# One token tile transposed by a DMA from ScalarE's queue, with six feature tiles ahead of it

## The chip, the cores and the metric

The kernel runs on one core of a Trainium2 chip. The core has five engines with instruction streams of their own: TensorE (PE in the profile; its weight loads are PEld), VectorE (DVE), ScalarE (ACT), GpSimd (POOL) and SyncE (SP). SyncE, ScalarE and GpSimd each have a queue from which they issue DMAs. The metric is the device time in microseconds, as a median over runs.

## The reference

The input x has 2048 tokens of 512 features. It is normalised per token, and the result goes through a diagonal state space layer and a gated feed-forward layer. Both are added to x:

```python
xn = _layernorm(x)
# A: state space layer, P = 512 complex states
Lam_bar = exp(dt * Lam);  B_bar = ((Lam_bar - 1) / Lam)[:, None] * Bmat
Bu = einsum("bld,pd->blp", xn, B_bar)
h[t] = Lam_bar * h[t-1] + Bu[t]
A = 2 * einsum("blp,dp->bld", h, Cmat).real + xn * Dskip
# B: feed-forward layer, F = 1376 hidden features
B = (silu(xn @ w_gate) * (xn @ w_up)) @ w_down
out = x + A + B
```

Inputs and output are bfloat16.

## The kernel before

**Tiling.** The 2048 tokens are 4 chunks of 512, and a chunk is 4 token tiles of 128 (`TPC`). The 512 input features are 4 slices of 128 (`KD`), called k. The hidden features are 11 feature tiles, called fi, the last with 96 rows. Matmuls read `xnT`, the normalised tokens with the features on the partitions, so each token tile has to be transposed after its normalisation. PSUM has eight banks of 512 columns, all handed out by `bank()`.

**Two ways to transpose.** `xT_pe(n)` takes four 128x128 transposes on TensorE (L231) into two banks, and two copies from there into `xnT` by VectorE (L238) or ScalarE (L240). `xT_dma(n)` issues one transposing DMA from SyncE's queue (L245). The kernel uses `xT_pe` for token tiles 0 to 3 and `xT_dma` for 4 to 15.

**The order of the work** is written out by hand; each engine runs its instructions in program order. The start loads x and the first weights in groups of feature tiles (0 to 1, 2, 3 to 6, 7 to 9) from SyncE's queue, L121 to L135; x of chunk 1 follows (L137). After that come the eight transposing DMAs of the state space input matrix, `BT` (L140), four for its real part and four for its imaginary part, one for each k; the weights of feature tiles 7 to 9 stand between the two parts (L112, called from L142 and L143), and the weights of the last feature tile behind (L145, L146).

On TensorE the first chunk goes as follows. Ten dummy matmuls (L653) come first. Then token tiles 0 to 3 are normalised one by one (`norm_dve`, L214, on VectorE; its scale comes from ScalarE, L202) and transposed, and `head_mm` (L676) multiplies the tiles that have arrived with feature tiles 0 to 2 into six held banks. With tile 3 these banks are complete; `gu_out` (L455, L456) empties each pair on ScalarE, the gate through Silu and the up product by a copy. Feature tiles 3 to 6 follow for all 512 tokens at once (`gateup_tile`, whose matmuls are L441). Then comes `bproj_tile`, the product of the chunk with `BT` (L366): the four 128-state tiles of the real part, and then those of the imaginary part, each with the matmuls of k = 0 to 3 in turn. Feature tiles 7 to 10 close the chunk's gate and up products. The later chunks follow with the same stages, and the output products with `w_down` and with the state space output matrix.

VectorE's longer work (tables of sines and cosines, statistics of later chunks, rotations, scans) lies in a backlog. `pump(us)` behind a group of matmuls takes from it about as much as fits into the given time. The products of gate and up for a pair of feature tiles (L460) are collected in `products`, and `multiply(keep)` issues them.

Of the kernel before, what the change touches and what calls it, by code (L numbers as in the profile page):

```python
# [11 lines left out]
BF16 = mybir.dt.bfloat16  # L12
ALU = mybir.AluOpType
ACT = mybir.ActivationFunctionType
# [9 lines left out]
def kernel(  # L24
# [17 lines left out]
    nc = tc.nc  # L42
    _, L, D = A_x.shape
    Pst = A_Lambda_re.shape[0]
    F = B_w_gate.shape[1]
    assert L % 512 == 0 and D % 128 == 0 and Pst % 128 == 0 and Pst == D
    CW = 512
# [3 lines left out]
    TPC = CW // 128  # L51
    KD = D // 128
    NQ = Pst // 128
    FT = (F + 127) // 128
    fsz = [min(128, F - i * 128) for i in range(FT)]
# [3 lines left out]
    LA, LB = 32, 64  # L59
    FL = (FT - 1) * 128  # L60
# [6 lines left out]
    up_p = ctx.enter_context(tc.tile_pool(name="up_p", bufs=4))  # L67
# [5 lines left out]
    def bank(shape=(128, CW), dtype=F32):  # L73
        return psum.tile(list(shape), dtype, name="ps")
# [4 lines left out]
    x_v = A_x[0].rearrange("(n p) d -> p n d", p=128)  # L79
    out_v = out[0].rearrange("(n p) d -> p n d", p=128)  # L80
    wg_v = B_w_gate.rearrange("(k p) f -> p k f", p=128)
    wu_v = B_w_up.rearrange("(k p) f -> p k f", p=128)


    xall = const.tile([128, NT, D], BF16, name="xall")
    xnT = const.tile([128, KD, L], BF16, name="xnT")

    fgroups = [(0, 2), (2, 3), (3, 7), (7, FT - 1)]
    wg_g, wu_g = [], []
# [4 lines left out]
    w_last = const.tile([128, KD, 128], BF16, name="w_last")  # L94
    wu_last = const.tile([128, KD, LB], BF16, name="wu_last")
    wd_sb = const.tile([128, FT - 1, D], BF16, name="wd_sb")
    BT = const.tile([128, 2, KD, Pst], BF16, name="BT")
# [6 lines left out]
    def wslice(groups, fi, k):  # L104
        for (a, b), t in zip(fgroups, groups):
            if a <= fi < b:
                return t[:, k, (fi - a) * 128:(fi - a) * 128 + fsz[fi]]


    def load_w1(q, tiles, view, gi):  # L110
        a, b = fgroups[gi]
        q.dma_start(out=tiles[gi][:], in_=view[:, :, a * 128:min(F, b * 128)])  # L112
# [20 lines left out]
        nc.gpsimd.dma_start(out=prm_rows[i * NQ:(i + 1) * NQ, :], in_=v.rearrange("(q j) -> q j", j=128))  # L133
    load_w1(nc.sync, wg_g, wg_v, 2)
    load_w1(nc.sync, wu_g, wu_v, 2)  # L135
    for n in (TPC, TPC + 2):
        nc.sync.dma_start(out=xall[:, n:n + 2, :], in_=x_v[:, n:n + 2, :])  # L137
    for part, src in enumerate((A_B_re, A_B_im)):
        for k in range(KD):
            nc.sync.dma_start_transpose(out=BT[:, part, k, :], in_=src[:, k * 128:(k + 1) * 128])  # L140
        if part == 0:
            load_w1(nc.sync, wg_g, wg_v, 3)  # L142
            load_w1(nc.sync, wu_g, wu_v, 3)  # L143

    nc.sync.dma_start(out=w_last[:, :, 0:LB + LA], in_=wg_v[:, :, FL:F])  # L145
    nc.sync.dma_start(out=w_last[:, :, LB + LA:128], in_=wu_v[:, :, FL + LB:F])  # L146

    def load_late():
        nc.sync.dma_start(out=wu_last[:], in_=wu_v[:, :, FL:FL + LB])
# [43 lines left out]
    def xn_tile(c):  # L193
        return xn_end if c == NCH - 1 else xall[:, c * TPC:(c + 1) * TPC, :]
# [17 lines left out]
    def norm_dve(n, lo=0, hi=D):  # L212
        c, i = divmod(n, TPC)
        nc.vector.tensor_scalar(out=xn_tile(c)[:, i, lo:hi], in0=xall[:, n, lo:hi], scalar1=mv[:, n, 0:1],  # L214
                                scalar2=rstd[:, n:n + 1], op0=ALU.subtract, op1=ALU.mult)
# [8 lines left out]
    def xT_pe(n, on_dve=(), prm_too=False):  # L224

        c, i = divmod(n, TPC)
        for h in range(2):
            tp = bank((128, HK * 128 + 128), BF16)
            for k in range(HK):
                lo = (h * HK + k) * 128  # L230
                nc.tensor.transpose(out=tp[:, k * 128:(k + 1) * 128], in_=xn_tile(c)[:, i, lo:lo + 128],  # L231
                                    identity=ident[:])
            if prm_too and h == 1:
                prm_transpose(tp[:, HK * 128:])
            dst = xnT[:, h * HK:(h + 1) * HK, n * 128:(n + 1) * 128]
            src = tp[:, 0:HK * 128].rearrange("p (k t) -> p k t", k=HK)
            if h in on_dve:
                nc.vector.tensor_copy(out=dst, in_=src)  # L238
            else:
                nc.scalar.copy(out=dst, in_=src)  # L240
        return tp[:, HK * 128:]

    def xT_dma(n):
        c, i = divmod(n, TPC)
        nc.sync.dma_start_transpose(out=xnT[:, :, n * 128:(n + 1) * 128], in_=xn_tile(c)[:, i, :])  # L245


    prm = const.tile([128, 3, NQ], F32, name="prm")
# [9 lines left out]
    V = nc.vector  # L258

    def prm_transpose(pp):  # L260
        nc.tensor.transpose(out=pp, in_=prm_rows[:], identity=ident[:])
# [173 lines left out]
    u_pair = {}  # L435
    products = []

    def gu_mm(ps, groups, c, fi, lo, hi):
        fs = fsz[fi]
        for k in range(KD):  # L440
            nc.tensor.matmul(ps[:fs, lo:hi], lhsT=wslice(groups, fi, k),  # L441
                             rhs=xnT[:, k, c * CW + lo:c * CW + hi], start=(k == 0), stop=(k == KD - 1))

    def gu_tile(c):
        if c not in gu_tiles:
            gu_tiles[c] = gut.tile([128, FT - 1, CW], BF16, name="guT")
        return gu_tiles[c]

    def gu_out(c, fi, psg, psu):

        guT = gu_tile(c)
        fs = fsz[fi]
        if fi % 2 == 0:
            u_pair[c] = up_p.tile([128, 2, CW], BF16, name="u2")
        nc.scalar.activation(out=guT[:fs, fi, :], in_=psg[:fs], func=ACT.Silu)  # L455
        nc.scalar.copy(out=u_pair[c][:fs, fi % 2, :], in_=psu[:fs])  # L456
        if fi % 2 == 1:
            lo = fi - fi % 2
            g, u = guT[:fs, lo:fi + 1, :], u_pair[c][:fs, 0:fi - lo + 1, :]
            products.append(lambda: V.tensor_tensor(out=g, in0=g, in1=u, op=ALU.mult))  # L460

    up_last = {}

# [40 lines left out]
    def gateup_tile(c, fi):  # L504
        if fi == FT - 1:
            return gateup_last(c)
        psg = bank()
        gu_mm(psg, wg_g, c, fi, 0, CW)
        psu = bank()
        gu_mm(psu, wu_g, c, fi, 0, CW)  # L510
        gu_out(c, fi, psg, psu)
# [97 lines left out]
    def queue(tag, ops, at=None):  # L609
        ops = [[op[0], op[1], op[2] if len(op) > 2 else None, tag] for op in ops]  # L610
        if at is None:
            backlog.extend(ops)
        else:
            backlog[at:at] = ops

    def step():
        for item in backlog[0:AHEAD + 1]:
            if item[2] is not None:
                item[2]()
                item[2] = None  # L620
        cost, op, _, _ = backlog.pop(0)
        op()
        owed[0] -= cost

    def pump(us):

        owed[0] += us
        while backlog and owed[0] >= backlog[0][0] * 0.5:
            step()
        if not backlog:  # L630
            owed[0] = 0.0

    def multiply(keep):

        while len(products) > keep:
            products.pop(0)()
            owed[0] -= 0.65
# [7 lines left out]
    GU = 8 * 0.2163  # L645
    BP = 4 * 0.2163
    H = 3
    held = [(bank(), bank()) for _ in range(H)]
# [6 lines left out]
    def ln_rest(c, on_act):  # L655
        ops = [(0.7, lambda n=n: ln_stats(n)) for n in range(c * TPC, (c + 1) * TPC)]
        def fin():
            ln_rstd(c * TPC, (c + 1) * TPC)
        def nbf():
            ln_nb(c * TPC, (c + 1) * TPC)  # L660
        ops += [(0.1, fin)]
        tail = [(0.1, nbf)] if on_act else []
        for n in range(c * TPC, (c + 1) * TPC):
            def one(n=n):
                (norm_act if on_act else norm_dve)(n)
                xT_dma(n)
            tail.append((0.05 if on_act else 0.35, one))
        return ops, tail
# [3 lines left out]
    def head_mm(which, lo, hi, ks, fis):  # L672

        for fi in fis:
            for k in ks:
                nc.tensor.matmul(held[fi][which][:, lo * 128:hi * 128], lhsT=wslice((wg_g, wu_g)[which], fi, k),  # L676
                                 rhs=xnT[:, k, lo * 128:hi * 128], start=(k == 0), stop=(k == KD - 1))

    allk = range(KD)
# [31 lines left out]
    params_a(pp)  # L711
    head_mm(1, 0, 2, allk, (2,))
    norm_dve(3)
    head_mm(0, 2, 3, range(0, HK), range(H))
    head_mm(1, 2, 3, range(0, HK), range(H))
    xT_pe(3, on_dve=(0, 1))
    head_mm(0, 2, 3, range(HK, KD), range(H))
    head_mm(1, 2, 3, range(HK, KD), range(H))
    tables = table_ops()
# [3 lines left out]
    queue("tables", tables[2:3])  # L723
    queue("ln1", norm1)
    queue("tables", tables[3:4] + [(0.1, params_sin)] + tables[4:])
    for fi in range(H):
        head_mm(0, 3, 4, allk, (fi,))
        head_mm(1, 3, 4, allk, (fi,))
        gu_out(0, fi, *held[fi])
        pump(GU / 4)  # L730
    pump(2.0)

    def bproj_chunk(c):
        need(f"ln{c}")
# [47 lines left out]
        queue(f"ssm{c}", fwd + back)  # L782

    G0 = 7
    for fi in range(H, G0):
        gateup_tile(0, fi)
        pump(GU)
        multiply(1)
# [72 lines left out]
```

## Time and profile before

| | |
|---|---|
| median of 3 runs | 178.56 us (178.43 to 178.92) |
| the profiled execution | 178.79 us, its span 177.0 us |
| TensorE busy | 173.4 us |
| VectorE busy | 154.0 us |
| ScalarE busy | 94.2 us |
| GpSimd busy | 51.3 us |
| DMA, mean over the span | 92 GB/s, 16.23 MB |

The span is the stretch in which instructions run; the profiled execution's own time is 1.8 us longer. Times in the traces are counted from the span's start. In a timeline a row merges consecutive instructions of one line; its columns are start, duration, engine, line, operation, tiles, shapes and count. SPq and ACTq are the queues from which SyncE and ScalarE issue DMAs. A matmul's duration includes its way through the array; the distance between starts is what one costs in a row of them.

### The profile page before, as it was taken

What the parts mean: (1) busy time and instruction counts of PE and PEld (TensorE: products, weight loads), DVE (VectorE), ACT (ScalarE), POOL (GpSimd) and SP (SyncE); (2) the same over time, 40 slices, a digit from 0 to 9 for tenths busy, and PEclk for the clock granted to TensorE, in tenths of its full rate; (3) what the DMA queues carried; (4) which work ended last, traced back from release to release, by engine and by line L of the source; (5) the groups of instructions that cost most, each with busy time, mean ns of one, the idle gap of its engine ahead of it and who ended that gap; (6) DMA issues with size and microseconds to landing.
All of it is one profiled execution on the core that took longest, in us unless ns stands there. A gap on an engine that the chain in (4) does not pass through costs nothing.

```text
span 177.0 us, 2543 instructions
## 1 busy us (share of the span) xinstructions
PE 173.4 (98%) x927; PEld 82.3 (46%) x927; DVE 154.0 (87%) x234; ACT 94.2 (53%) x167; POOL 51.3 (29%) x85
## 2 busy tenths in 40 slices
PE   8999999999999999999999999999999999999993
PEld 2984444444444444444444444444444444444443
DVE  3789997999999996899999999999999999993033
ACT  3468898967299649923766661053866610001300
POOL 6050300000300050003999640058185250001410
PEclk9999999999999999999999999999999999999999
DMA  5998745996141016900000020019659600000662
GB/s 169 279 297 215 141 88 122 361 206 111 22 88 31 4 28 117 348 11 2 20 17 19 15 67 24 4 17 132 88 78 178 116 9 0 0 0 6 63 99 74
DMA packets 30764, 16.23 MB, mean 92 GB/s; under 512 B 19680, under 2 KB 30560, under 8 KB 30720
## 3 DMA queue, kind: packets, MB, share of 16 engines
q1 hardware_dynamic: 24704, 11.44, 27.9%
q0 software_dynamic: 5184, 4.07, 16.0%
q10 hardware_dynamic: 864, 0.56, 1.0%
q8 instruction: 7, 0.11, 0.3%
q14 instruction: 5, 0.04, 0.1%
HBM read 8.33 MB, written 5.24 MB: 77 GB/s over the span
## 4 chain that ended last, share of the span: by engine, by line
PE 96%; DMA 1%; DVE 1%; issue 0%
PE ps L441 36%; PE ps L587 16%; PE ps L366 16%; PE ps L575 10%; PE ps L549 10%; PE ps L676 3%; PE ps L496 2%; PE ps L538 2%; DMA xall<-in_A_x_dram 1%; PE ps L485 1%; PE ps L231 1%; DVE stats L197 0%; PE ps L653 0%; DVE xall L214 0%; DVE stats L684 0%; DVE res L592 0%
## 5 line engine op out<-in xcount | busy, mean ns | idle before, releaser
L441 PE MATMUL ps<-xnT,wu 128*128 128x512 bf16 x148 | 38.0, 379 | 0.0
L441 PE MATMUL ps<-xnT,wg 128*128 128x512 bf16 x148 | 38.0, 379 | 0.0
L408 DVE TENSOR_TENSOR_SCAN g<-r_t,car,u 128x512 bf16<-128x512 f32 x24 | 28.7, 1260 | 0.0
L455 ACT ACTIVATE guT<-ps 128x512 bf16<-128x512 f32 x40 | 24.4, 611 | 7.3 <-PE ps L441 5.5
L366 PE MATMUL ps<-xnT,BT 128*128 128x512 bf16 x128 | 28.3, 379 | 0.0
L587 PE MATMUL ps<-CF,wt 128*128 128x512 bf16 (+2 forms) x144 | 28.2, 356 | 0.0
L456 ACT CAST u<-ps 128x512 bf16<-128x512 f32 x40 | 23.9, 598 | 5.6 <-PE ps L441 5.6
L600 ACT CAST res<-ps 128x512 bf16<-128x512 f32 x12 | 6.7, 590 | 36.0 <-PE ps L587 26.8
L181 POOL DMA_DIRECT2D gu_rows<-ul x36 | 17.6, 498 | 18.1 <-DVE ul L473 18.1
L441 PEld LDWEIGHTS <-wu 128*128 128x128 bf16 x148 | 14.5, 98 | 17.4
L441 PEld LDWEIGHTS <-wg 128*128 128x128 bf16 x148 | 14.4, 98 | 17.2
L368 ACT CAST u<-ps 128x512 bf16<-128x512 f32 x32 | 18.4, 591 | 5.1 <-PE ps L366 4.9
L601 POOL DMA_DIRECT2D out_dram<-res x12 | 10.6, 1224 | 34.3 <-ACT res L600 34.2
L587 PEld LDWEIGHTS <-wt 128*128 128x128 bf16 x144 | 13.3, 98 | 15.0 <-issue 0.8
L366 PEld LDWEIGHTS <-BT 128*128 128x128 bf16 x128 | 12.5, 98 | 15.1
L206 POOL TENSOR_TENSOR rstd<-ve,neg_half 128x4 f32<-128x4 f32 x3 | 5.2, 1730 | 47.0 <-DVE ve L205 47.0
L575 PE MATMUL ps<-wd_sb,guT 128*128 128x512 bf16 x80 | 17.6, 379 | 0.0
L549 PE MATMUL ps<-wd_sb,guT 128*128 128x512 bf16 x80 | 17.4, 379 | 0.0
L460 DVE TENSOR_TENSOR guT<-guT,u 128x1024 bf16<-128x1024 bf16 x20 | 13.5, 678 | 0.0
L575 PEld LDWEIGHTS <-guT 128*128 128x128 bf16 x80 | 7.8, 98 | 9.4
L549 PEld LDWEIGHTS <-guT 128*128 128x128 bf16 x80 | 7.8, 98 | 9.5
L197 DVE BATCH_NORM_STATS2 stats<-xall 128x6 f32<-128x512 bf16 x14 | 9.5, 677 | 1.9 <-DMA xall<-in_A_x_dram 1.9
(114 smaller groups left out, 194.7 us busy)
## 6 DMA issues: line engine op xcount, KB each, us to landing
out_dram<-in_A_x_dram SPq DMA_DIRECT2D x1, 1536.0 KB, 7.1
out_dram<-res POOLq DMA_DIRECT2D x12, 128.0 KB, 3.5
out_dram<-xall POOLq DMA_DIRECT2D x3, 512.0 KB, 7.6
wd_sb<-in_B_w_down_dram SPq DMA_DIRECT2D x2, 640.0 KB, 9.0
xall<-in_A_x_dram SPq DMA_DIRECT2D x1, 1024.0 KB, 7.2
gu_rows<-ul POOLq DMA_DIRECT2D x36, 8.0 KB, 1.6
wg<-in_B_w_gate_dram SPq DMA_DIRECT2D x1, 512.0 KB, 5.0
wu<-in_B_w_up_dram SPq DMA_DIRECT2D x1, 512.0 KB, 6.1
```

The lines of the kernel that those rows point to most:

```text
L181: nc.gpsimd.dma_start(out=gu_rows[c][i * RT:(i + 1) * RT, p, :], in_=product[p * RT:(p + 1) * RT, i * 128:(i + 1) * 128])
L366: nc.tensor.matmul(ps[:], lhsT=BT[:, part, k, q * 128:(q + 1) * 128], rhs=xnT[:, k, c * CW:(c + 1) * CW], start=(k == 0), stop=(k == KD - 1))
L368: nc.scalar.copy(out=u_tiles[c][:, part, q, :], in_=ps[:])
L408: V.tensor_tensor_scan(out=g()[:, part, q, :], data0=r_t[:, q:q + 1].to_broadcast([128, CW]), data1=u_tiles[c][:, part, q, :], initial=ini ...
L441: nc.tensor.matmul(ps[:fs, lo:hi], lhsT=wslice(groups, fi, k), rhs=xnT[:, k, c * CW + lo:c * CW + hi], start=(k == 0), stop=(k == KD - 1))
L455: nc.scalar.activation(out=guT[:fs, fi, :], in_=psg[:fs], func=ACT.Silu)
L456: nc.scalar.copy(out=u_pair[c][:fs, fi % 2, :], in_=psu[:fs])
L460: products.append(lambda: V.tensor_tensor(out=g, in0=g, in1=u, op=ALU.mult))
L549: nc.tensor.matmul(o[:], lhsT=gu_tiles[k][:, fi, i * 128:(i + 1) * 128], rhs=wd_sb[:, fi, :], start=(fi == 0), stop=False)
L575: nc.tensor.matmul(o[:], lhsT=gu_tiles[c][:, fi, i * 128:(i + 1) * 128], rhs=wd_sb[:, fi, lo:hi], start=(fi == 0), stop=False)
L587: nc.tensor.matmul(o, lhsT=w_tiles[c][:, part, q, i * 128:(i + 1) * 128], rhs=CF[:, part, q, lo:hi], start=(fresh and part == 0 and q == 0 ...
L601: nc.gpsimd.dma_start(out=out_v[:, n, :], in_=res[:], accum_op=ALU.add)
```

## The change

Token tile 3 is no longer transposed by TensorE and copied by VectorE, but by one transposing DMA from ScalarE's queue. Feature tiles 0 to 5 (instead of 0 to 2) are multiplied with the first three token tiles, 384 columns, and their banks are emptied in this width. Then token tile 3 is multiplied with the same six feature tiles, four of them together in one bank each for gate and up, and two in a third bank; `end_out` empties these, and the products of the three pairs follow. The remaining feature tile 6 and the product with `BT` come after that as before.

The DMAs of `BT`, of the weights of feature tiles 7 to 9, and of the last feature tile's weights are put in a function, `load_mid`, which is called behind the transposing DMA of tile 3. They stay on SyncE's queue. The two loads of x for chunk 1 become one.

```diff
-    for n in (TPC, TPC + 2):
-        nc.sync.dma_start(out=xall[:, n:n + 2, :], in_=x_v[:, n:n + 2, :])
-    for part, src in enumerate((A_B_re, A_B_im)):
...
+    nc.sync.dma_start(out=xall[:, TPC:2 * TPC, :], in_=x_v[:, TPC:2 * TPC, :])
+
+    def load_mid():
+        for part, src in enumerate((A_B_re, A_B_im)):
+            for k in range(KD):
+                nc.sync.dma_start_transpose(out=BT[:, part, k, :], in_=src[:, k * 128:(k + 1) * 128])
+            if part == 0:
+                load_w1(nc.sync, wg_g, wg_v, 3)
+                load_w1(nc.sync, wu_g, wu_v, 3)
+        nc.sync.dma_start(out=w_last[:, :, 0:LB + LA], in_=wg_v[:, :, FL:F])
+        nc.sync.dma_start(out=w_last[:, :, LB + LA:128], in_=wu_v[:, :, FL + LB:F])
...
-    def xT_dma(n):
+    def xT_dma(n, q=nc.sync):
         c, i = divmod(n, TPC)
-        nc.sync.dma_start_transpose(out=xnT[:, :, n * 128:(n + 1) * 128], in_=xn_tile(c)[:, i, :])
+        q.dma_start_transpose(out=xnT[:, :, n * 128:(n + 1) * 128], in_=xn_tile(c)[:, i, :])
...
+    def gu_out(c, fi, psg, psu, hi=CW):
+
+        nc.scalar.activation(out=gu_tile(c)[:, fi, 0:hi], in_=psg[:, 0:hi], func=ACT.Silu)
+        nc.scalar.copy(out=u_tile(c, fi)[:, fi % 2, 0:hi], in_=psu[:, 0:hi])
+        if fi % 2 == 1 and hi == CW:
+            product(c, fi)
...
     norm_dve(3)
+    xT_dma(3, nc.scalar)
+    load_mid()
     head_mm(0, 2, 3, range(0, HK), range(H))
     head_mm(1, 2, 3, range(0, HK), range(H))
-    xT_pe(3, on_dve=(0, 1))
     head_mm(0, 2, 3, range(HK, KD), range(H))
     head_mm(1, 2, 3, range(HK, KD), range(H))
...
+    EARLY = 2 * H
+    EC = (TPC - 1) * 128
     for fi in range(H):
-        head_mm(0, 3, 4, allk, (fi,))
-        head_mm(1, 3, 4, allk, (fi,))
-        gu_out(0, fi, *held[fi])
-        pump(GU / 4)
-    pump(2.0)
+        gu_out(0, fi, *held[fi], hi=EC)
+    psg = [bank() for fi in range(H, EARLY)]
+    for fi in range(H, EARLY):
+        gu_mm(psg[fi - H], wg_g, 0, fi, 0, EC)
+        pump(GU * 3 / 8)
+    for fi in range(H, EARLY):
+        psu = bank()
+        gu_mm(psu, wu_g, 0, fi, 0, EC)
+        gu_out(0, fi, psg[fi - H], psu, hi=EC)
+        pump(GU * 3 / 8)
+
+    def end_mm(ps, at, groups, fi):
+        for k in range(KD):
+            nc.tensor.matmul(ps[:, at * 128:(at + 1) * 128], lhsT=wslice(groups, fi, k), rhs=xnT[:, k, EC:CW],
+                             start=(k == 0), stop=(k == KD - 1))
+
+    def end_out(fis, psg, psu):
+        guT = gu_tile(0)
+        nc.scalar.activation(out=guT[:, fis[0]:fis[-1] + 1, EC:CW],
+                             in_=psg.rearrange("p (f t) -> p f t", t=128), func=ACT.Silu)
+        for i in range(0, len(fis), 2):
+            nc.scalar.copy(out=u_tile(0, fis[i])[:, :, EC:CW],
+                           in_=psu[:, i * 128:(i + 2) * 128].rearrange("p (f t) -> p f t", t=128))
+            product(0, fis[i + 1])
+
+    psg, psu = bank(), bank()
+    for ps, groups in ((psg, wg_g), (psu, wu_g)):
+        for fi in range(4):
+            end_mm(ps, fi, groups, fi)
+    end_out(range(4), psg[:], psu[:])
+    pump(GU)
+    multiply(1)
+    ps = bank()
+    for i, groups in enumerate((wg_g, wu_g)):
+        for fi in range(4, EARLY):
+            end_mm(ps, 2 * i + fi - 4, groups, fi)
+    end_out(range(4, EARLY), ps[:, 0:256], ps[:, 256:512])
+    pump(GU / 2)
+    multiply(1)
...
-    for fi in range(H, G0):
+    for fi in range(EARLY, G0):
         gateup_tile(0, fi)
```

More of the change, by code (lines that the diff above doesn't have):

```diff
@@ L135 @@
     load_w1(nc.sync, wu_g, wu_v, 2)
-    for n in (TPC, TPC + 2):
-        nc.sync.dma_start(out=xall[:, n:n + 2, :], in_=x_v[:, n:n + 2, :])
-    for part, src in enumerate((A_B_re, A_B_im)):
[L139 to L146, printed above, removed]
+    nc.sync.dma_start(out=xall[:, TPC:2 * TPC, :], in_=x_v[:, TPC:2 * TPC, :])
[8 more added lines that the diff above has]
+        nc.sync.dma_start(out=w_last[:, :, LB + LA:128], in_=wu_v[:, :, FL + LB:F])
     def load_late():
@@ L447, in gu_tile, with u_tile, product @@
         return gu_tiles[c]
[L449 to L460, printed above, removed]
+    def u_tile(c, fi):
+        if (c, fi // 2) not in u_pair:
+            u_pair[c, fi // 2] = up_p.tile([128, 2, CW], BF16, name="u2")
+        return u_pair[c, fi // 2]
+    def product(c, fi):
+        g, u = gu_tile(c)[:, fi - 1:fi + 1, :], u_tile(c, fi)[:]
+        products.append(lambda: V.tensor_tensor(out=g, in0=g, in1=u, op=ALU.mult))
+    def gu_out(c, fi, psg, psu, hi=CW):
[3 more added lines that the diff above has]
+            product(c, fi)
     up_last = {}
```

## The prediction

> **What bounds the kernel now.** I read the page's busy table first, then the chain that ended last, then TensorE's timeline over the first chunk, then the timeline of SyncE's DMA queue, and last the landing times of each transposing DMA.
>
> ```profile
> span 177.0 us, 2543 instructions
> PE 173.4 (98%) x927; PEld 82.3 (46%) x927; DVE 154.0 (87%) x234; ACT 94.2 (53%) x167; POOL 51.3 (29%) x85
> ...
> PE 96%; DMA 1%; DVE 1%; issue 0%
> ```
>
> TensorE is busy for 98% of the span and is 96% of the chain. In the chain in order of time its pieces follow each other from 4.62 to 174.26 us without a gap. So a saving counts only if it shortens TensorE's own work, and any wait that TensorE gets is added in full, since nothing later can take it back. The stage is read here:
>
> ```profile
> 9.36 0.50 PE L676 MATMUL ps<-xnT,wu 128*128 128x128 bf16 x6
> 9.70 0.39 PE L231 MATMUL ps<-ident,xall 128*128 128x128 bf16 x4
> 9.92 0.50 PE L676 MATMUL ps<-xnT,wg 128*128 128x128 bf16 x6
> ...
> 11.93 1.03 PE L441 MATMUL ps<-xnT,wg 128*128 128x512 bf16 x4
> ...
> 18.84 7.07 PE L366 MATMUL ps<-xnT,BT 128*128 128x512 bf16 x32
> ```
>
> The columns are start, duration, engine, line, operation, tiles, shape and count. The four transposes of token tile 3 (L231) sit between matmuls and cost 9.92 - 9.70 = 0.22 us of TensorE. At 18.84 the product with BT begins: 16 matmuls for the real part, 16 for the imaginary part, 0.216 us apart, so the imaginary part starts at 18.84 + 3.46 = 22.30. Within it the first tile takes the four k slices in turn, so the fourth slice of BT's imaginary part is first read at 22.30 + 0.65 = 22.95. BT comes through SyncE's queue:
>
> ```profile
> 7.03 5.37 SPq L140 DMA_TRANSPOSE BT<-in_A_B_re_dram  x4
> 12.45 0.58 SPq L112 DMA_DIRECT2D wg<-in_B_w_gate_dram  x1
> 13.08 1.14 SPq L112 DMA_DIRECT2D wu<-in_B_w_up_dram  x1
> 14.26 5.09 SPq L140 DMA_TRANSPOSE BT<-in_A_B_im_dram  x4
> ```
>
> A transposing DMA holds the queue for 1.3 us each. The fourth imaginary one is issued at 18.07 and lands 3.0 us later (the shortest of these eight landings, which lie between 3.0 and 6.5 us), at 21.07. So BT has only 22.95 - 21.07 = 1.88 us to spare. That is the number on which this change turns.
>
> **The change part by part.**
>
> *TensorE's work.* Removed: four transposes, 0.22 us. Split: features 3 to 5 go from 24 matmuls of 512 columns (0.216 us apart) to 24 of 384 and 24 of 128. The trace has 128 columns at 0.056 us apart and 256 columns at 0.108 (four from 7.88 to 8.31); 384 isn't there and lies between 0.108 and 0.216, on the straight line at 0.162. The pair costs 0.218 against 0.216, times 24 is 0.05 us. Features 0 to 2 keep their 24 small matmuls, only later. Sum: -0.22 + 0.05 = -0.17 us. Unhindered, the product with BT would start at 18.67.
>
> *Weights and banks.* Features 3 to 5 are now read from 10.37 (the end of tile 2's matmuls without the transposes) instead of 11.93. Their gate weights are issued at 4.26 and land 5.0 later, their up weights at 4.82 and 6.1 later: 9.3 and 10.9, and up is needed only at 10.37 + 12 x 0.162 = 12.3. Cost nothing; cover 1.1 us or more. The third new bank needs the first of the held ones emptied; ScalarE can begin that at about 10.85 (below), 0.4 us each, and TensorE asks at 11.67. Cost nothing with 0.4 us of cover. If that cover is gone, a wait of up to 1 us appears here, and it is hidden behind the later wait on BT.
>
> *ScalarE.* The transposing DMA now stands in ScalarE's queue and waits there for the normalisation of tile 3 (DVE L214, 9.11 to 9.52), so I put its issue at 9.6. Behind it stand only the evictions of features 0 to 2; the table load before it ends at 9.38. Its issue takes 1.2 us by L245, and the evictions start at 10.85 against 11.02 before. Twelve evictions of 512 columns become 12 of 384 and 5 longer or shorter ones: the same columns, five more starts. A start is 0.12 us by the 256 and 512 column evictions (0.36 and 0.60 us), 0.6 us in all, in a stage where ScalarE has 6.84 - 5.90 = 0.94 us free (12.0 to 18.84). Nothing on the path.
>
> *VectorE* loses two copies of L238 (0.49 us together). It isn't on the chain. Three products wait until tile 3 is done, about 16.7 instead of 16.0; behind them stand the statistics of chunk 1, needed much later. Nothing.
>
> *Tile 3 itself.* Issue 9.6, landing by the nearest rows, the twelve transposing DMAs of other tiles at L245: 2.4 median, 3.1 at most. It arrives at 12.0 to 12.7. TensorE needs it only after six features, at 10.37 + 24 x 0.162 = 14.27. Hidden, with 1.6 us or more of cover.
>
> *The eight BT transposes, the last weights behind them (L145, L146), and all else on SyncE's queue.* The function that issues them now stands behind the ScalarE transpose in the program. Before has transposes on SyncE's queue only, so its trace can't show whether the first of SyncE's waits for ScalarE's, and until when. Three ends: no wait (issue at about 6.5, after one shorter x load); until it is issued (10.85); until it has landed (12.0 to 12.7). I take the landing: waits on a DMA in this page end at its landing (VectorE's 1.9 us at L197 on the x load). From then the queue is taken as before: first BT issue to last landing was 21.07 - 7.03 = 14.04 us. Two terms of it can shrink without the crowd of loads that it met at 7 to 12 us: four issues 5.09 instead of 5.37, and the up weights' issue 0.51 (as at 4.82) instead of 1.14. The ends are thus 14.04 and 13.13; I take 13.44, the first term in full and half of the second. So the last slice lands at 12.0 + 0.1 + 13.44 = 25.54. The wait passes the two weight loads of group 3 too (needed at 25.75 before, landed about 5 us after an issue near 17.5: covered) and the transposes of chunk 1 (last issue then about 29, landing 31.5, needed at 31.79 plus the delay: covered by the delay itself).
>
> The Trainium skill, DMA: Bandwidth & Descriptors, section "Silent corruption: two transposing streams in flight at once", says that transposes from SyncE's and ScalarE's queues must not be in flight together, and that the later stream's first has to wait for the earlier one's full completion. By that rule the release is the landing and the sum stays +2.6; with a release at the issue it would be +1.4; no trace here shows either.
>
> *The sum.* After the last slice lands, TensorE has the last matmul of the first tile and twelve more to do, 13 x 0.216 = 2.81 us; the part then ends at 25.54 + 2.81 = 28.35, against 25.75 before: +2.6 us. The real part's fourth slice (issued 12.1 + 3 x 1.27 = 15.9, landing at 18.9 by 3.0 us) is needed at 18.67 + 0.65 = 19.3, so it adds nothing. The 0.17 us saved is spent inside the wait. Profiled execution: 178.79 + 2.6 = 181.4; it stood 0.23 above the median of 178.56, so the median is forecast at 181.2. Ends of this case: 13.13 us of queue gives +2.3; 14.04 and a tile 3 landing of 3.1 gives 26.85, +3.9. That is 180.9 to 182.5.
>
> **The rivals.**
>
> *The wait also cools TensorE's clock.* For: the kernel starts slow after idleness, eight matmuls of 128 columns from 5.45 to 6.25, 0.10 us apart, then 0.056, although the granted clock reads 1.00 throughout; half speed lasts from 0.78 to about 6.25. Against: the slices land 1.27 us apart, so single matmuls break the wait into pieces. Price: half speed for between 3.4 us (as long as the wait itself, 22.1 to 25.5) and the 5.4 us of the start, half of each lost: 1.7 to 2.7. Time 181.2 + 2.2 = 183.4.
> The Trainium skill, TensorE: Matmul & The Clock Gate, section "Part 1: The HAM clock gate (the "warmup" mystery)", has the clock halved after an idle window of about 3.4 us; the slow start here agrees, and no run shows a pause within the kernel.
>
> *SyncE's queue isn't held to the landing.* Released at the issue of the ScalarE transpose: 180.0. Not held at all: BT is as early as before, the slack of 1.88 us covers it, and only -0.17 is left, 178.4, no change that can be measured. The turn lies at a first BT issue of 7.03 + 1.88 = 8.9 to 9.8 us (with the 0.91 shorter queue): later costs, earlier is free. For: nothing in BT's data needs tile 3. Against: the transpose is released only by an event at 9.52, and even its issue ends past 9.8. This is the end on the other side, not slower; faster by over 0.3%, 0.54 us, would need more than the 0.22 us of removed work, and I find no row that gives it.
>
> *ScalarE gets late with its extra starts and TensorE waits for banks.* Up to 1 us between 10.4 and 18.7, but all of it ahead of the wait on BT's last slice, which ends at 25.54 whenever TensorE arrives: 181.2 all the same.
>
> **How the numbers follow.** TensorE waits for BT, clock unchanged: 0.68 (the bank rival in it). The same with a slow clock: 0.14. Released at the issue: 0.06. Not held: 0.10. Something unseen: 0.02. About 0.3% is what a measurement of this kernel can tell from no change. Slower collects the first three, 0.88. Not held gives same 0.08 and faster 0.02; the unseen is halved between these: same 0.09, faster 0.03. The range takes the main case, the early release and most of the slow clock: 179.7 to 184.0.
>
> **What would show it.** SyncE's timeline: first BT transpose at about 12.1 instead of 7.03, the last near 22.5. TensorE's timeline: a new gap before the imaginary part of L366 at 22.1, matmuls one by one until about 25.5, then 0.216 us apart; 0.106 or 0.43 us would mean the slow clock. From 14.3 on small matmuls for tile 3 without a gap before them. After 40 us every stage is late by the same amount. Wrong if BT's first transpose is issued before 9.8, or if TensorE is idle before 18 us by more than 3 us.

## The result, and the profile after

The change made the kernel slower: 192.78 us (192.17 to 193.95, 6 runs) against 178.43 us, a ratio of 1.0803 (95% interval 1.0769 to 1.0837). The ratios, here and below, are taken over the fast runs (one of the four runs of the first experiment, 187.66 us, is slow and left out) and aren't quotients of the two medians. The forecast was 181.2 us with a range to 184.0. The direction was right, the loss more than five times the forecast one. The page of the changed kernel, its span, its busy row of TensorE and its chain by engine:

```profile
span 191.1 us, 2590 instructions
PE 175.3 (92%) x947; PEld 83.4 (44%) x947; DVE 153.5 (80%) x232; ACT 95.4 (50%) x172; POOL 51.4 (27%) x85
...
PE 62%; DVE 17%; SPq 9%; ACT 4%; DMA 3%; issue 2%; POOL 1%; ACTq 1%
```

TensorE's work has hardly changed, but it is only 62% of the chain now, and SyncE's queue, which wasn't in the chain before, has 9%. VectorE's 17% isn't time lost: at 87.50 us TensorE has one wait of 0.26 us for a transpose of chunk 3, and the chain goes from there back through VectorE's backlog. TensorE's timeline of the first chunk (the bracket is the idle time before the row and what ended it):

```profile
9.98 1.46 PE L441 MATMUL ps<-xnT,wg 128*128 128x384 bf16 x8
23.05 1.44 PE L441 MATMUL ps<-xnT,wg 128*128 128x384 bf16 x4 [11.61 <-ACT guT L460]
24.29 3.79 PE L441 MATMUL ps<-xnT,wu 128*128 128x384 bf16 x12
27.91 1.06 PE L746 MATMUL ps<-xnT,wg 128*128 128x128 bf16 x16
...
32.32 7.07 PE L366 MATMUL ps<-xnT,BT 128*128 128x512 bf16 x32
```

The eight matmuls of two gate groups find banks; the third group waits 11.61 us for ScalarE to empty one. The sixteen matmuls behind the wait then take 4.86 us to 27.91 where 16 x 0.162 = 2.59 us was the price. The product with BT, in which the forecast had put its wait, runs through without one. Why ScalarE was late is told by the chain in order of time (start, duration, what), which here follows the waits back:

```profile
14.50 1.18 SPq L141
...
17.03 1.26 SPq L141
...
18.33 2.58 DMA BT<-in_A_B_im_dram
20.91 0.02 issue
...
21.17 1.29 ACTq L245
22.46 0.05 issue
22.51 0.50 ACT guT L460
23.01 0.04 issue
23.05 5.02 PE ps L441 x16
```

The last imaginary transpose of BT is issued from SyncE's queue at 18.33 and lands at 20.91; right behind that ScalarE issues its transpose of tile 3, at 21.17, and only then starts to empty banks. In ScalarE's timeline the releaser named for this wait is another one, a load of the last weights, which the second experiment takes up:

```profile
21.17 1.29 ACTq L245 DMA_TRANSPOSE xnT<-xall  x1
22.51 0.49 ACT L460 ACTIVATE guT<-ps 128x384 bf16<-128x384 f32 x1 [13.36 <-DMA w_last<-in_B_w_gate_dram]
```

SyncE's own timeline shows that it waited for nothing of tile 3:

```profile
6.10 6.21 SPq L141 DMA_TRANSPOSE BT<-in_A_B_re_dram  x4
12.36 1.55 SPq L112 DMA_DIRECT2D wg<-in_B_w_gate_dram  x1
13.96 0.50 SPq L112 DMA_DIRECT2D wu<-in_B_w_up_dram  x1
14.50 5.09 SPq L141 DMA_TRANSPOSE BT<-in_A_B_im_dram  x4
```

So one queue's transposes do wait for the other's, but in the opposite direction to the one assumed: ScalarE waits for SyncE. BT is as early as before, and tile 3, with every eviction queued behind it, is 11.6 us later than forecast. The wait is in the program as built, where this instruction stands behind all eight transposes of BT, although its call comes ahead of theirs. It carries these waits (DMAHW are eight semaphores that count landings of the DMAs of SyncE's and ScalarE's queues, each used in turn for every eighth DMA; DMAHW1 to 4 belong to the four imaginary transposes, 5 and 6 to the last two real ones):

```
L245 DmaTransposeAnt xnT<-xall 128x4x128 [waits DMAHW4_49,DMAHW3_49,DMAHW5_49,DMAHW2_49,DMAHW6_49,DMAHW1_49,DVE_49]
```

The clock, from the busy time by stretch (the stretch, then busy time of PE, PEld, DVE, ACT and POOL, then the granted clock, DMA share and GB/s):

```profile
12.00:19.00 7.00, 0.00 (x0) 0.00 (x0) 4.34 (x9) 0.00 (x0) 0.00 (x0) 0.64 1.21 222
19.00:26.00 7.00, 2.95 (x10) 1.39 (x10) 0.00 (x0) 2.98 (x8) 0.00 (x0) 0.50 0.33 62
26.00:30.00 4.00, 4.00 (x46) 2.96 (x45) 0.00 (x0) 2.73 (x7) 0.00 (x0) 0.79 0.00 0
30.00:34.00 4.00, 4.00 (x30) 2.16 (x28) 3.56 (x8) 2.96 (x7) 1.30 (x1) 1.00 0.00 0
```

In the wait the granted clock falls to 0.50, at about 14.0 us by finer stretches, and it is back at 1.00 only by 28 us (0.66 from 27 to 28, 1.00 from 28 to 29). The time up to the start of BT's product adds up: wait from 11.28 (where the next matmul was due) to 23.05, 11.77; slow matmuls, 4.86 - 2.59 = 2.27; removed work, -0.17; an earlier start of the first feature tiles in this execution (third gate group due 0.39 us earlier than the forecast's count), -0.39. Sum 13.48, and 32.32 - 18.84 = 13.48. Up to the span's end it grows to 14.1; what lies behind BT's product is taken up with the new order below.

### The profile page after: what moved, and what is told of

The parts are those of the page before. It is cut to its first block, busy times and chain, and to the rows that moved or that the text cites. A ratio compares the mean times of both kernels' runs of the same rounds, so it can differ in the third digit from the quotient of the medians.

```text
span 191.1 us, 2590 instructions
## 1 busy us (share of the span) xinstructions
PE 175.3 (92%) x947; PEld 83.4 (44%) x947; DVE 153.5 (80%) x232; ACT 95.4 (50%) x172; POOL 51.4 (27%) x85
## 3 DMA queue, kind: packets, MB, share of 16 engines
q1 hardware_dynamic: 24688, 11.44, 25.8%
## 4 chain that ended last, share of the span: by engine, by line
PE 62%; DVE 17%; SPq 9%; ACT 4%; DMA 3%; issue 2%; POOL 1%; ACTq 1%
PE ps L441 23%; PE ps L590 15%; PE ps L552 9%; PE ps L366 7%; SPq L141 5%; DVE g L408 5%; PE ps L578 5%; DVE pm L376 4%; SPq L112 3%; DVE stats L197 3%; DVE guT L456 2%; PE ps L541 1%; PE ps L746 1%; DMA BT<-in_A_B_im_dram 1%; DMA xnT<-xn_end 1%
## 5 line engine op out<-in xcount | busy, mean ns | idle before, releaser
L441 PE MATMUL ps<-xnT,wg 128*128 128x512 bf16 (+1 forms) x148 | 37.8, 380 | 11.6 <-ACT guT L460 11.6
L441 PE MATMUL ps<-xnT,wu 128*128 128x512 bf16 (+1 forms) x148 | 38.7, 389 | 0.0
L460 ACT ACTIVATE guT<-ps 128x512 bf16<-128x512 f32 (+1 forms) x40 | 23.7, 591 | 19.1 <-DMA w_last<-in_B_w_gate_dram 13.4
L461 ACT CAST u<-ps 128x512 bf16<-128x512 f32 (+1 forms) x40 | 23.1, 578 | 6.8 <-PE ps L441 6.7
L456 DVE TENSOR_TENSOR guT<-guT,u 128x1024 bf16<-128x1024 bf16 x20 | 13.4, 679 | 13.8 <-ACT u L754 13.8
L441 PEld LDWEIGHTS <-wu 128*128 128x128 bf16 x148 | 15.1, 102 | 18.1 <-issue 2.1
L368 ACT CAST u<-ps 128x512 bf16<-128x512 f32 x32 | 18.5, 589 | 6.3 <-PE ps L366 6.3
L366 PEld LDWEIGHTS <-BT 128*128 128x128 bf16 x128 | 12.5, 98 | 15.2 <-issue 0.3
L376 DVE TENSOR_TENSOR pm<-u,c 128x2048 bf16<-128x2048 bf16 x8 | 9.8, 1220 | 2.0 <-ACT c L305 1.9
```

Of the source, the lines that this page charges most:

```text
L366: nc.tensor.matmul(ps[:], lhsT=BT[:, part, k, q * 128:(q + 1) * 128], rhs=xnT[:, k, c * CW:(c + 1) * CW], start=(k == 0), stop=(k == KD - 1))
L368: nc.scalar.copy(out=u_tiles[c][:, part, q, :], in_=ps[:])
L376: V.tensor_tensor(out=t[:], in0=flat(src()[:, i]), in1=flat(tab[:]), op=ALU.mult)
L460: nc.scalar.activation(out=gu_tile(c)[:, fi, 0:hi], in_=psg[:, 0:hi], func=ACT.Silu)
L461: nc.scalar.copy(out=u_tile(c, fi)[:, fi % 2, 0:hi], in_=psu[:, 0:hi])
```

## The experiments

**BT without transposes.** Leaves out the transposition of BT, so that the state space part differs from the reference.

```diff
-                nc.sync.dma_start_transpose(out=BT[:, part, k, :], in_=src[:, k * 128:(k + 1) * 128])
+                nc.sync.dma_start(out=BT[:, part, k, :], in_=src[k * 128:(k + 1) * 128, :])
```

> The changed kernel with BT loaded by plain DMAs of its rows, not transposed (the state space part of the output is therefore not the reference's). It leaves ScalarE's transpose of tile 3 as the only transpose until chunk 1. Theory A: in the changed kernel that transpose waits for the last transpose of BT on SyncE's queue to land. Then its issue moves from 21.17 to 9.5 to 12 us here, TensorE has no gap of several us before 18 us, and the time is 178.2 to 179. Rival B: it waits for SyncE's queue to run empty, down to the loads of the last weights (the page names w_last as the releaser). These loads stay, so the issue comes at about 16 us or later, TensorE still has a gap of some 5 us, and the time is 184 to 188.

Measured 186.35 us (ratio 1.0413, 1.037 to 1.0456). Its ScalarE timeline:

```profile
14.41 1.34 ACTq L245 DMA_TRANSPOSE xnT<-xall  x1
15.80 0.49 ACT L460 ACTIVATE guT<-ps 128x384 bf16<-128x384 f32 x1 [6.48 <-DVE stats L197]
```

The issue moved forward by 6.8 us, but not to 10, so theory A's number failed. The time and TensorE's gap of 4.61 us are those of rival B, but its mechanism isn't: at 14.41 the w_last loads aren't yet issued (14.74 and 15.94). The built program has one DMA wait left on this instruction, the semaphore whose turn it is; its last user was the third real load of BT, issued at 7.74, which lands about 6.5 us later in the crowd of loads, at 14.3. So a second wait was under the first one: the reuse of a landing semaphore. This run couldn't by itself name the first one.

**The last weights ahead of BT.**

```diff
     def load_mid():
+        nc.sync.dma_start(out=w_last[:, :, 0:LB + LA], in_=wg_v[:, :, FL:F])
+        nc.sync.dma_start(out=w_last[:, :, LB + LA:128], in_=wu_v[:, :, FL + LB:F])
         for part, src in enumerate((A_B_re, A_B_im)):
...
-        nc.sync.dma_start(out=w_last[:, :, 0:LB + LA], in_=wg_v[:, :, FL:F])
-        nc.sync.dma_start(out=w_last[:, :, LB + LA:128], in_=wu_v[:, :, FL + LB:F])
```

> The changed kernel with the two loads of the last feature tile's weights (w_last) issued ahead of BT instead of behind it. In the built program ScalarE's transpose of tile 3 then stands between the third and the fourth imaginary transpose of BT. Theory A: ScalarE waits until the transposes of BT that stand ahead of it have landed: BT is 1.1 us later in the queue, its third imaginary slice lands at about 21, ScalarE issues at 21 to 21.7 as in the changed kernel: 192 to 193.5 us. Rival B: it waits for w_last, as the page's releaser says: w_last lands by 13, the issue comes before 18 and the time is under 189.

Measured 194.6 us (1.0907, 1.0892 to 1.0922). ScalarE's issue, and the third and the fourth imaginary transposes of BT in SyncE's timeline:

```profile
23.58 1.28 ACTq L245 DMA_TRANSPOSE xnT<-xall  x1
...
20.34 1.26 SPq L143 DMA_TRANSPOSE BT<-in_A_B_im_dram  x1
...
26.09 1.12 SPq L143 DMA_TRANSPOSE BT<-in_A_B_im_dram  x1
```

The third goes out at 20.34 and lands 3.0 us later by the list of DMA issues, at 23.34; ScalarE issues 0.24 us behind it (0.26 in the changed kernel). Tile 3 lands 2.5 us after its issue, at 26.08, and the fourth goes out at 26.09: the two queues alternate, each waiting for the other's landing. The w_last loads had landed by 14.2. Rival B is out: the page's releaser of the changed kernel, "DMA w_last", was only the nearest event. Theory A holds in its mechanism; the issue came 1.9 us later than its numbers and the time is 1.1 us above its range, since BT's own transposes took longer (four real ones 7.58 us).

**Evictions ahead of the issue.** The call of `xT_dma(3, nc.scalar)` moves behind the loop with the evictions of feature tiles 3 to 5.

> The changed kernel with the issue of tile 3's DMA moved in ScalarE's queue behind the twelve evictions of 384 columns; it still comes from ScalarE and still waits. This parts the two costs of the wait: evictions queued behind it, and tile 3 being late. Theory A: the issue stays at about 21.2 and tile 3 lands at 23.7; TensorE no longer stops at 11.6 but runs to about 13.9, stops there for 9.8 us, and does the 48 small matmuls at half speed: about 190.5 to 191.5, 1 to 2 us less than the changed kernel. Rival D: the blocked evictions are nearly all of the cost, the transpose itself could go earlier: below 184.

Measured 191.35 us (1.0715, 1.0698 to 1.0732). TensorE's timeline:

```profile
12.01 2.11 PE L441 MATMUL ps<-xnT,wu 128*128 128x384 bf16 x12
24.19 1.89 PE L746 MATMUL ps<-xnT,wg 128*128 128x128 bf16 x16 [10.06 <-DMA xnT<-xall]
```

As theory A had it: with the banks free TensorE runs on to 14 us and then waits 10.06 us for tile 3 itself, which was issued at 21.65. The blocked evictions are worth 1.4 us, or 1.9 us if the issue, which came 0.48 us later in this execution than in the changed kernel's, is allowed for; nearly all of the rest goes with the late transpose. Behind the wait the 128-column matmuls come 0.105 us apart instead of 0.056.

**TensorE kept busy in the wait.**

```diff
+    for _ in range(48):
+        nc.tensor.matmul(psg[0][:], lhsT=ones[:, 0:128], rhs=ones[:], start=True, stop=True)
     for fi in range(H, EARLY):
         gu_mm(psg[fi - H], wg_g, 0, fi, 0, EC)
```

> The changed kernel with 48 matmuls on constants put ahead of feature tile 3, in a bank that the gate overwrites right after: they keep TensorE busy for 10.4 of the 11.6 us of its wait and are over before ScalarE frees the bank. Theory F: after the wait the changed kernel runs at half speed for about 5 us and loses 2.4 us to it; here the matmuls behind the wait are 0.162 us apart at once and the time is 190.2 to 190.7. Rival G: the slow matmuls behind the wait are the evictions' doing, not the clock's: 192.5 to 193.

Measured 191.23 us (1.0705, 1.0683 to 1.0726). That is 0.5 us above theory F's range; in the profiled execution ScalarE's issue came 0.50 us later (21.67). TensorE's timeline:

```profile
20.67 1.46 PE L441 MATMUL ps<-xnT,wg 128*128 128x384 bf16 x8
23.53 0.81 PE L441 MATMUL ps<-xnT,wg 128*128 128x384 bf16 x4 [1.40 <-ACT guT L460]
24.18 2.11 PE L441 MATMUL ps<-xnT,wu 128*128 128x384 bf16 x12
```

Four gate matmuls take 0.65 us to the next row, full speed at once, and BT's product starts at 30.53 instead of 32.32: 1.79 + 0.50 = 2.29 us gained, the 2.27 us that the sum above gives the clock. Theory F holds. The Trainium skill, TensorE: Matmul & The Clock Gate, section "Part 1: The HAM clock gate (the "warmup" mystery)", has the clock halved after an idle window of about 3.4 us. The granted 0.50 agrees; the fall came about 2.6 us after the last matmul's end in the changed kernel (11.44 to 14.0) and 4.2 us in the run before this one (14.13 to 18.3).

**The assumed direction made real.**

```diff
     xT_dma(3, nc.scalar)
+    nc.sync.dma_start(out=gu_rows[3][:, 0, :], in_=xnT[:, 0, 3 * 128:4 * 128])
     load_mid()
```

> The changed kernel with one small DMA (128x128, of tile 3's xnT into a tile that is written again later) on SyncE's queue ahead of BT. It can't be issued before tile 3 has landed, so BT is behind tile 3 and ScalarE's transpose finds no other transpose ahead of it: this is the order that the prediction assumed. Theory A (the prediction's sum was wrong in the direction of the wait, not in its arithmetic): ScalarE issues at 9.3 to 9.7, tile 3 lands at 12 to 13.7, BT is issued from 12.6 to 14.3 and its last slice lands 13.8 us later (as measured with tile 3 on SyncE's queue); with 0.8 us for the later stage that the new order alone showed, 182.2 to 185. Rival E: ScalarE's transposing DMA is slow by itself or ScalarE is blocked whatever stands ahead: over 188.

Measured 184.69 us (1.0372, 1.0325 to 1.0418). SyncE's queue, and TensorE in BT's product:

```profile
13.75 0.57 SPq L718 DMA_DIRECT2D gu_rows<-xnT  x1
14.36 5.18 SPq L141 DMA_TRANSPOSE BT<-in_A_B_re_dram  x4
...
20.95 2.98 PE L366 MATMUL ps<-xnT,BT 128*128 128x512 bf16 x13 [0.81 <-DMA BT<-in_A_B_re_dram]
25.22 0.39 PE L366 MATMUL ps<-xnT,BT 128*128 128x512 bf16 x1 [1.29 <-DMA BT<-in_A_B_im_dram]
26.21 0.39 PE L366 MATMUL ps<-xnT,BT 128*128 128x512 bf16 x1 [0.60 <-DMA BT<-in_A_B_im_dram]
26.84 3.50 PE L366 MATMUL ps<-xnT,BT 128*128 128x512 bf16 x14 [0.24 <-DMA BT<-in_A_B_im_dram]
```

This is the profile that the prediction described: single matmuls as BT's slices land, and in this execution no slow clock (1.00 from 12 to 30 us). Of the four runs one, 186.69 us, has a mean granted clock of 0.991, so there it did fall; where isn't known. ScalarE issues at 9.08; the transpose lands 4.7 us later instead of 2.4, the real part is late too, and the added copy takes 0.6 us. The product with BT ends at 30.18 instead of 25.75, 4.43 us of the loss. The time is within theory A's range; rival E is out. BT itself was quicker than theory A had it: 12.5 us from its first issue to the last matmul group (14.36 to 26.84), not 13.8.

**Tile 3 on SyncE's queue.** `xT_dma(3, nc.scalar)` becomes `xT_dma(3)`.

> The changed kernel with the one transposing DMA of tile 3 issued from SyncE's queue, ahead of BT, and all else as changed. Theory A: with one queue nothing waits for the other queue's landings; SyncE waits for the normalisation, issues tile 3 at about 9.6 and BT from 10.9. By the prediction's chain of 13.4 us the last slice of BT lands at 24.4, 1.4 us after it is needed: 179.9 us (179.5 to 180.6), with TensorE's only gap before the imaginary part of BT. Rival C: the new order with six feature tiles and 17 evictions is itself what costs: then the gap after two gate matmul groups remains, and the time is above 185.

Measured 181.08 us (1.0137, 1.0122 to 1.0153), 0.5 us above theory A's range. SyncE's queue, and TensorE in BT's imaginary part:

```profile
9.28 1.31 SPq L245 DMA_TRANSPOSE xnT<-xall  x1
10.64 5.66 SPq L141 DMA_TRANSPOSE BT<-in_A_B_re_dram  x4
...
24.48 2.98 PE L366 MATMUL ps<-xnT,BT 128*128 128x512 bf16 x13 [0.37 <-DMA BT<-in_A_B_im_dram]
27.30 1.03 PE L441 MATMUL ps<-xnT,wg 128*128 128x512 bf16 x4
```

TensorE's only gaps between 10 and 40 us are those of BT's imaginary part, which ends at 27.30 instead of 25.75: 1.55 us, where 1.4 was forecast. Rival C's gap is not there. About 1 us more appears later, which the next two runs take up.

**The new order alone.** TensorE transposes tile 3 as before; the order, the evictions and the single x load stay as changed.

> The changed kernel with tile 3 transposed by TensorE and copied by VectorE as before; the new order (six feature tiles in 384 columns, then tile 3 with six) and the single x load stay. Theory A: the order costs only 0.05 us of TensorE: 178.5, no change. Rival C: the order with its extra evictions and its bank use makes TensorE wait: over 179.5.

Measured 179.3 us (1.0041, 1.0029 to 1.0054): small, but not nothing, against theory A. BT's product starts at 18.59, not late. The loss comes at 73 us, in the up product of the last feature tile, here in this run and then in the kernel before:

```profile
72.31 1.27 PE L488 MATMUL ps<-xnT,wu_last 128*64 128x512 bf16 x9
73.81 1.02 PE L488 MATMUL ps<-xnT,wu_last 128*64 128x512 bf16 x7 [0.24 <-DMA xnT<-xn_end]
74.77 7.08 PE L590 MATMUL ps<-CF,wt 128*128 128x512 bf16 x32
...
72.46 1.92 PE L485 MATMUL ps<-xnT,wu_last 128*64 128x512 bf16 x16
74.31 7.08 PE L587 MATMUL ps<-CF,wt 128*128 128x512 bf16 x32
```

The sixteen matmuls take 2.46 us to the next row instead of 1.85: 0.61 us. (The bracket's 0.24 counts only from the modelled end of the matmul before.)

**The order with the pump put back.** The change had also dropped a `pump(2.0)`, which takes 2 us of VectorE's backlog early.

```diff
         gu_out(0, fi, *held[fi], hi=EC)
+    pump(2.0)
```

> The kernel with the new order and TensorE's transpose (179.3 us), with the pump of 2.0 us that the change dropped put back behind the evictions of the held banks. Theory H: the 0.8 us that the new order cost come from VectorE's backlog being taken 2 us later, so that chunk 3's transposes are late for the up matmuls at 73 us: 178.3 to 178.6 here, without TensorE's wait at 73 us. Rival I: they come from the five more evictions or the bank order: 179.2 as before.

Measured 178.56 us (1.0008, 0.9999 to 1.0016), and no wait at 73 us. Theory H holds: the order is free; taking the backlog later made the transposes of chunk 3 late. The first of them is issued at 66.96 us without the pump and at 65.03 with it.

**Both together.** Tile 3 on SyncE's queue, with the pump.

> The kernel with tile 3 on SyncE's queue ahead of BT (181.08 us), with the pump of 2.0 us put back. Theory H: 0.8 us of its 2.6 us were the backlog taken late; what stays is TensorE's wait of 1.55 us for the last slice of BT, less 0.1: 179.9 to 180.3. Rival K: the wait for BT is all of the 2.6 us: 181.1 as before.

Measured 180.73 us (1.0126, 1.0112 to 1.0139): between H and K. The late wait is gone, but BT's imaginary part ended 0.17 us later in the profiled execution, and TensorE waited 0.30 us for feature tile 3's gate weights at 10.49. By the medians the pump is worth 0.35 us here, less than the 0.74 us of the pair before, and the intervals of the two ratios overlap (1.0122 to 1.0153 without it), so that it helps on the whole isn't shown in this pair.

**Tile 3 between BT's transposes.** The order on SyncE's queue: half of x for chunk 1, two real transposes of BT, tile 3, the other half of x, the rest of BT as before; with the pump.

> An attempt at a version that beats both: tile 3 transposed by a DMA from SyncE's queue, put between the second and the third real transpose of BT so that SyncE's idle 3 us ahead of the normalisation are used; x of chunk 1 is loaded in two halves, the second behind tile 3; the pump of 2.0 us is back. Theory A: the first two transposes of BT are issued before tile 3 is normalised, the last slice of BT lands 2 us earlier than with tile 3 ahead of all BT (24.45), at about 22.4, just ahead of its need at 22.8. TensorE saves its 0.17 us: 178.2 to 178.4, which is at the edge of what can be told. Rival J: tile 3 now lands behind two slices of BT, 1 us later than the 13.6 measured with it ahead, and TensorE waits for it at 14: 178.8 to 179.5.

Measured 179.86 us (1.0085, 1.007 to 1.01). TensorE waits for tile 3:

```profile
14.81 1.07 PE L750 MATMUL ps<-xnT,wg 128*128 128x128 bf16 x16 [0.45 <-DMA xnT<-xall]
```

Rival J's mechanism: issued at 9.61, tile 3 lands 5.2 us later; the time is 0.4 us above J's range. BT's product has no wait, and it starts 0.39 us late (19.23). TensorE stays that late to its last stage (160.60 instead of 160.22), and another 0.5 us of the profiled execution lies behind the issue of the last store (at 174.99 instead of 174.60; the span ends at 177.9 instead of 177.0). The rest of the 1.4 us isn't accounted for. No version here beats the kernel before.

## Why the prediction was right or wrong

- **The bound** was right: TensorE is gapless before, and no wait of the changed kernel was taken back later.
- **The rule on two queues** was the right thing to weigh, and was used half. The step that failed is the one on BT's eight transposes, and with it ScalarE's issue at 9.6: of the three ends of the wait one was no wait, and the other two were ends of a wait of SyncE for ScalarE. The other direction wasn't among the rivals. It could have been priced from the rows shown: last BT landing 21.07, so ScalarE's issue at about 21.1 instead of 9.6; measured 21.17. BT was in fact not held at all, which the forecast took for the harmless case (178.4 us). Both of the prediction's signs of being wrong came: BT's first issue ahead of 9.8 (6.10), and TensorE idle by more than 3 us ahead of 18 us (from 11.4). That the kernel came out slower, as forecast, is luck: the wait that was forecast did not happen. The argument used was the order of calls in the program text. But nothing holds BT's transposes back: the first is out at 6.10, before tile 3 is normalised, and in the built program tile 3 is the one that waits. With BT put later in the queue its fourth imaginary transpose did wait for tile 3, and with a DMA on SyncE's queue that needs tile 3 all eight did; in the built programs tile 3 stands ahead of just these. That fits an order by readiness; how the program is ordered when it is built was not tested further.
- **ScalarE and the banks:** "if that cover is gone, a wait of up to 1 us" was the right place, but the cover was lost by 11.6 us, not 1. All that stood behind the waiting issue on ScalarE waited with it: the first eviction starts at 22.51, 0.05 us after the issue is over. Splitting it, 1.4 to 1.9 us are due to the evictions and some 0.7 to the dropped pump; the rest goes with tile 3 itself, the slow clock behind the wait included.
- **Tile 3's landing** was mis-sized: 2.4 to 3.1 us from transposes later in the kernel; beside the first loads it was 4.3 to 5.2. In the changed kernel, at 21.17, it was 2.5.
- **BT's chain** of 13.44 us was about right: 13.8 us with tile 3 on SyncE's queue (10.64 to the last matmul group at 24.48), 12.5 us when issued from 14.36 (`sync_waits`). The predicted mechanism, made real, costs 6.2 us instead of 2.6: tile 3's late landing and the added copy put BT's first issue at 14.36 instead of 12.1, the real part waits too, and the pump is missing.
- **The clock** was a rival for the wrong wait. In waits of up to 1.29 us between single matmuls (`sync_waits`) the granted clock stayed at 1.00 in the profiled execution; in a wait of 11.6 us it fell, which cost 2.3 us.
- **The order** was right at about nothing (178.56 with the pump), but a term was missing: the dropped `pump(2.0)`, 0.74 us.

## What to carry to other kernels

When a change puts on a second queue a kind of transfer of which only one queue's may be under way at a time, as with the transposing DMAs of these programs, ask for both directions which one waits, and price each; here the one whose inputs came late was the one that waited. A DMA issue on a computing engine is an instruction in that engine's order: list what stands behind it before costing its wait at nothing. And the waits of 4.6 us and more in which TensorE was idle as a whole cost more than their length here, while in the profiled execution the one broken up by single matmuls didn't.

## What the runs showed of the hardware

- A transposing DMA of one token tile took 2.5 us to land behind the crowd of loads (ScalarE's queue, at 21.17) and 4.3 to 5.2 us beside the first loads (4.7 from ScalarE's queue, 4.3 to 5.2 from SyncE's).
- After the 11.6 us wait TensorE ran at the granted 0.50 for about 4.6 us from its restart (23.05 to about 27.7). A wait of 4.61 us, in the run with plain loads of BT, brought the clock down too: 0.50 from 16 to 20 us.
- Removing one wait of a DMA can uncover another that was hidden under it: with no transposes ahead, ScalarE's issue still waited for the landing semaphore of an earlier load, until 14.41.
